# Two output tiles of one chunk stored by one transfer, and a hand-written instruction order replaced by another

## The chip, the cores and the metric

The kernel runs on one core of one Trainium2 chip. A core has TensorE (matmuls and transposes, called PE in the profile; PEld is its loading of weights), VectorE (DVE), ScalarE (ACT), GpSimd (POOL) and SyncE (SP), each with an instruction stream of its own, and 16 DMA engines that all queues share. The metric is the time of the core on the device in microseconds (us), the median over the runs. Before the change it is 308.44 us.

## The reference

It is causal attention over a sliding window, followed by a two-layer network. Cut to what is computed:

```python
# q, k, v: (8 batches, 8 heads, 576 tokens, 64), float32
scores = q @ k.transpose / 8
scores = where(0 <= row - column < 64, scores, -1e9)
attn   = exp(scores - max) / sum            # softmax over columns
y      = attn @ v
x      = y as (8 * 576 = 4608 tokens, 8 * 64 = 512)
h      = x @ w_in                           # 512 x 2048
g      = h - tanh(h)
out    = g @ w_out                          # 2048 x 512, out is (4608, 512) float32
```

## The kernel before

**Tiling.** A batch has 576 tokens, which are nine windows of 64; a window's queries look at 128 keys, its own and those of the window ahead. Heads are taken in pairs: a *group* g is batch g // 4 and pair g % 4, so groups 0 to 3 are batch 0 and groups 4 to 7 are batch 1. The network works on nine *chunks* of 512 tokens, so chunk 0 needs batch 0 alone, and the network of one chunk runs on TensorE between the attention of later batches. All matmul operands are bf16 and all sums are float32. PSUM is one tile `ps` of eight banks, and each step of the program names the bank that it uses.

**The order.** Nothing is scheduled by a planner: the kernel turns automatic scheduling off and plays one long string of words, `PLAN`, from left to right. `play` splits a word at its dots and calls the helper that `STEPS` gives for it. So the string fixes the order of instructions on every engine and in every DMA queue; what waits for what between engines follows from which helper reads or writes which tile, and of two words whose spans of a tile overlap the later one in the string waits for the earlier one. The words that matter here, with g a group, c a chunk, and a final `.a`, `.v`, `.p` or `.s` for ScalarE, VectorE, GpSimd or SyncE:

- `lq.g`, `lk.g` (L107): load the q or k rows of one group; `.p` goes through GpSimd's queue, `.s` through SyncE's. `LV.b.i` (L142) loads 128 value rows of batch b with all heads, `lv` one head's value rows, `wi` and `wo` weights of the two layers; all these go through GpSimd's queue.
- `cq.g`, `ck.g` (`move`, L87 on ScalarE and L89 on VectorE): cast and reorder a group's rows to bf16.
- `Ep.g.bank`, `Fp.g.bank`: transpose q or k of a group on TensorE into a bank, in six matmuls where the rows were cast before (L252) and in twelve where not (L248). `Ec`, `Fc`: copy the result out of PSUM, on ScalarE or VectorE.
- `U.n.bank` (L219): n warm-up matmuls on a tile of zeros, whose result nobody reads; 512 columns wide, in bank 7 only 384.
- `Rp.g.grp.bank`: scores of a group for its first five (grp 0) or last four (grp 1) windows, into two banks. For groups 0 to 3 two matmuls that write the mask come first (L273). Bank 4 here stands for the banks 4 and 7. `Rx` is the exp of them on ScalarE (L310).
- `Z.b` (L148 and L149): two copies on VectorE by which value rows cross to the other half of the partitions; the weighted sums read them.
- `P.g` (L327): weighted sums of a group of batch 0, which also give the softmax's denominators; they lie in banks 5 and 6, for group 2 in banks 0 and 1. `D.g` (L367 and L369) is the reciprocal and the product that divide them; `DS` and `DH` are the same in parts for group 2. From batch 1 on two groups go together: `PP` (L340), `DR` and `DN`.
- `Xp`, `Xc` (L389 and `move`): transpose the divided sums on TensorE to the layout of a token chunk, and copy them out.
- `Hp` (L495) and `H` (L423): the first layer, 128 of the 2048 hidden columns at a time, in two halves of two matmuls or in four matmuls at once; `A` the tanh (L431, ScalarE), `G` the subtraction (L437, VectorE), `W` the second layer (L466; L459 for the last 128 tokens).
- `O.c.s` (`y_out`): copy 128 tokens' outputs of chunk c out of PSUM into a tile `ysb`, and store them with a transfer on SyncE's queue (L482). The last 128 tokens go in two parts, 384 and 128 columns wide (L477).

SyncE issues 105 transfers: two loads of rows (`lq.0.s`, `lk.0.s`), 66 DMA transposes of later batches, and 37 outputs. They use eight completion counters in turn, number n the counter (n - 1) mod 8, so that transfer 105 is on counter 0 and transfer 104 on counter 7; a transfer waits for the one eight before it, whose counter it takes over. At the end of the program SyncE waits for GpSimd's queues, then for its own counters 0 to 7 in this order, one instruction for each, and only then the program drains and ends (L633).

Of the kernel before, what the change touches and what calls it, by code (L numbers as in the profile page):

```python
# [15 lines left out]
def kernel(  # L16
# [68 lines left out]
    def move(eng, o, i):
        if eng is nc.scalar:
            nc.scalar.activation(o, i, ACT.Copy)  # L87
# [381 lines left out]
    def y_out(c, s, eng):  # L469
        if c == NC or (c, s) == (NC - 1, 3):  # L470
            half = c - NC + 1
            c, s = NC - 1, 3
# [4 lines left out]
            nc.sync.dma_start(out=out[r0:r0 + 128, d], in_=ysb[:, d])  # L477
# [41 lines left out]
    def play(script):  # L519
# [15 lines left out]
        Fc.6.4.v H.0.3 Ec.5.5.a cq.6.v Ep.6.5 G.0.1 Fc.5.3.a N A.0.3 Ec.6.5.v G.0.3 Rp.4.0.6 Rp.5.1.3 Hp.0.2.1  # L535
        lv.1.0.1 H.0.4 ck.8.v wi.4 Rx.5.1.3 A.0.2 A.0.4 Rx.4.0.6 G.0.2 H.0.6 H.0.5 A.0.6 Rp.6.1.4 mz Rp.6.0.5
        lq.8.p G.0.4 cq.7.v lv.1.3.1 A.0.5 zb.1.1.p lt.1 wo.0 H.0.7 Rx.6.1.4 zb.1.0.p Ep.7.3 Rx.6.0.5 Fp.7.4
        lv.1.2.0 lv.1.3.0 Rp.5.0.5 wo.2 A.0.7 G.0.5 H.0.8 M.4 G.0.6 H.0.9 G.0.7 za.1.1.p H.0.10 Ec.7.3.a
        Rx.5.0.5 Fc.7.4.v lk.9.p A.0.8 G.0.8 A.0.9 za.1.0.a H.0.11 A.0.10 Fp.8.5 A.0.11 Rp.7.1.3 M.6 G.0.9
        Rp.7.0.6 Rx.7.0.6 H.0.12 Fc.8.5.a G.0.10 G.0.11 wo.3 A.0.12 H.0.14 cq.8.v Ep.8.1 M.5 PP.4 G.0.12 A.0.14  # L540
        H.0.15 G.0.14 Ec.8.1.a A.0.15 DR.4 Rx.7.1.3 DN.4.0 H.0.13 DN.4.1 G.0.15 W.0.0.0 DN.4.2 M.7 za.1.2.a
        zb.1.2.v zb.1.3.p Rp.8.0.3 Rp.8.1.5 A.0.13 Rx.8.1.5 W.0.1.0 wo.1 lq.10.p lk.10.p lq.11.p za.1.3.v
        lk.11.p PP.6 G.0.13 cq.9.v Rx.8.0.3 LV.2.0 DR.6 Xp.1.0.0.3 lr.3.2 Xp.1.0.1.4 qr.3.3 W.0.1.2 Xc.1.0.1.4.v
        DN.6.1 W.0.0.2 Xc.1.0.0.3.a ck.9.v DN.6.0 DN.6.2 Fp.9.3 Hp.1.0.0 Ep.9.4 Xp.1.1.0.6 Xp.1.1.1.7 Fc.9.3.a
# [10 lines left out]
        qr.4.1 LV.3.4 Xc.2.0.1.3.a A.1.14 DN.10.0 W.1.0.0 G.1.14 LV.4.3 lr.4.1 W.1.0.2 A.1.15 Xp.2.1.1.4
        Xp.2.1.0.6 LV.4.2 W.1.0.1 LV.4.0 G.1.15 W.1.0.3 Xc.2.1.1.4.a Xc.2.1.0.6.a lr.4.0 qr.5.3 Hp.2.0.0
        Hp.2.0.1 A.2.0 qr.4.4 qr.5.4 H.2.3 tk.4.4 lr.6.4 qr.4.0 O.1.0.v A.2.3 W.1.1.3 G.2.3 W.1.1.2 lr.4.2
        Hp.2.1.1 Hp.2.1.0 G.2.0 lr.5.4 lr.5.2 H.2.2 qr.4.3 lr.4.3 A.2.1 S.12 W.1.1.0 LV.4.4 A.2.2 G.2.1 tq.4.4
        H.2.5 G.2.2 W.1.1.1 Sx.12.2 tq.4.0 Sx.12.1 Sx.12.0 A.2.5 Z.3 M.12 H.2.4 M.13 O.1.1.a A.2.4 qr.4.2 G.2.5
        PP.12 W.1.2.3 tq.4.1 tk.4.1 DR.12 G.2.4 tk.4.0 tk.4.2 DN.12.1 DN.12.2 H.2.7 DN.12.0 tk.4.3 tq.4.3 lr.6.3  # L560
        qr.5.2 lr.5.3 lr.5.0 H.2.6 S.14 lr.5.1 qr.5.0 qr.6.4 A.2.7 A.2.6 G.2.7 qr.6.0 H.2.9 Sx.14.2 Sx.14.0
        tq.4.2 A.2.9 Sx.14.1 G.2.6 G.2.9 M.14 W.1.2.2 W.1.2.1 W.1.2.0 H.2.8 H.2.11 M.15 A.2.8 G.2.8 PP.14
        Xp.3.0.0.4 A.2.11 DR.14 O.1.2.v H.2.10 Xp.3.0.1.3 W.1.3.3 W.1.3.2 A.2.10 DN.14.0 DN.14.1 G.2.10 G.2.11
        DN.14.2 H.2.12 A.2.12 H.2.13 W.1.3.0 W.1.3.1 A.2.13 Xp.3.1.1.7 G.2.12 G.2.13 H.2.15 Xp.3.1.0.6 O.1.3.a
        Xc.3.0.0.4.a H.2.14 Xc.3.1.1.7.a A.2.15 A.2.14 W.2.0.2 G.2.14 Xc.3.1.0.6.v G.2.15 W.2.0.0 W.2.0.1
        Xc.3.0.1.3.a tq.5.3 tq.5.4 tk.5.4 tz.4.v tq.5.2 Hp.3.0.1 W.2.0.3 Hp.3.1.1 Hp.3.1.0 O.2.0.a A.3.1 W.2.1.1
        Hp.3.0.0 W.2.1.2 G.3.1 A.3.0 S.16 Z.4 Sx.16.1 Sx.16.2 G.3.0 Sx.16.0 M.17 M.16 H.3.3 W.2.1.3 W.2.1.0
        H.3.2 A.3.3 PP.16 G.3.3 O.2.1.a DR.16 A.3.2 qr.5.1 H.3.5 LV.5.3 tk.5.2 G.3.2 DN.16.2 DN.16.0 tk.5.1
        tk.5.3 DN.16.1 tq.5.0 A.3.5 W.2.2.1 Y.4.0 H.3.4 S.18 A.3.4 Sx.18.0 G.3.5 H.3.7 G.3.4 A.3.7 G.3.7 Sx.18.1
        Sx.18.2 H.3.6 A.3.6 W.2.2.3 W.2.2.0 M.19 H.3.9 W.2.2.2 tk.6.4 tq.5.1 tk.5.0 G.3.6 qr.7.1 M.18 H.3.8  # L570
        A.3.9 PP.18 A.3.8 O.2.2.v G.3.9 DR.18 G.3.8 DN.18.2 DN.18.0 W.2.3.0 H.3.11 qr.6.2 DN.18.1 LV.5.4 A.3.11
        lr.6.2 W.2.3.3 W.2.3.1 H.3.10 W.2.3.2 A.3.10 G.3.11 G.3.10 Y.4.1 lr.6.0 tq.6.4 tq.6.2 O.2.3.a H.3.13
        H.3.14 A.3.13 LV.5.0 LV.5.1 LV.5.2 W.3.0.2 lr.6.1 qr.6.1 G.3.13 H.3.15 tz.5.v A.3.14 G.3.14 qr.6.3
        H.3.12 W.3.0.0 A.3.15 G.3.15 Hp.4.1.0 A.3.12 G.3.12 Hp.4.1.1 A.4.1 Hp.4.0.1 W.3.0.1 G.4.1 W.3.0.3 H.4.3
# [63 lines left out]
```

## Time and profile before

| | us |
|---|---|
| median of three runs | 308.44 |
| the three runs | 307.77, 308.44, 308.54 |
| the profiled execution | 308.71 |
| span of its profile (first to last instruction) | 307.0 |
| TensorE, matmuls busy | 298.4 |
| VectorE busy | 176.4 |
| ScalarE busy | 155.6 |
| GpSimd busy | 104.3 |

The granted clock of TensorE is 0.998 of full speed in the mean over the profiled execution. TensorE's matmuls cover 97% of the span. The largest groups of its time are the second layer's matmuls, 130.1 us, and the first layer's, 120.9 us and 20.9 us for those in halves; the 35 warm-ups are 10.8 us.

The rows that follow below have these forms. A row of the timeline gives the start, the busy time of the run of equal instructions, the engine, the line of the kernel, the operation, written tile <- read tiles, the shapes, and how many there are; the bracket is the idle time of that engine ahead of them and what ended it. A row of the windows gives the bounds of a stretch, its length, and each engine's busy time in it with the number of instructions, then TensorE's granted clock, the mean share of DMA engines in use (above 1 where transfers queue), and the rate in GB/s. In a row of a view of groups stand the count, the shortest, median and longest single time in ns, and the first and last start.

### The profile page before, as it was taken

The numbers are of one execution on the slowest core, as the hardware profiler recorded it, in microseconds if no ns is written. First come the engines' busy times: TensorE is split into PE (matmuls) and PEld (weight loads), VectorE is DVE, ScalarE is ACT, GpSimd is POOL, SyncE is SP. The second block draws the span as 40 slices with busy tenths as digits, with TensorE's granted clock in tenths as the row PEclk, the third lists the DMA queues.
The fourth block names the chain that finished last, engine by engine and source line by source line (L and its number), as shares of the span: only waits on it lengthen the run. The fifth ranks groups of instructions, "written<-read, shape, count | busy, mean of one in ns | idle before, by whom it ended". The sixth has DMA issues, their size and how long they took to land.

```text
span 307.0 us, 6473 instructions
## 1 busy us (share of the span) xinstructions
PE 298.4 (97%) x2599; PEld 149.5 (49%) x2632; DVE 176.4 (57%) x312; ACT 155.6 (51%) x263; POOL 104.3 (34%) x141
## 2 busy tenths in 40 slices
PE   8989999999999999999999999999999999999995
PEld 3555555455555545444544445444544444444443
DVE  1378995389577636765386575576663645355300
ACT  2668983577665356634464645345733433433202
POOL 8988756830979092038005870000000000000000
PEclk9999999999999999999999999999999999999999
DMA  8999999998999999969999999650032000001102
GB/s 161 153 191 193 186 192 176 160 188 123 115 150 136 176 154 138 184 108 144 178 139 125 144 173 128 144 99 34 36 75 73 35 36 34 34 34 36 67 35 104
DMA packets 132894, 36.77 MB, mean 120 GB/s; under 512 B 119936, under 2 KB 127360, under 8 KB 132864
## 3 DMA queue, kind: packets, MB, share of 16 engines
q0 software_dynamic: 92752, 18.06, 82.3%
q1 hardware_dynamic: 40112, 18.30, 30.9%
q8 instruction: 20, 0.33, 0.5%
q14 instruction: 10, 0.08, 0.1%
...
## 4 chain that ended last, share of the span: by engine, by line
PE 90%; DVE 2%; DMA 2%; POOL 2%; issue 1%; ACT 1%; DVEq 0%; ACTq 0%; POOLq 0%
PE ps L466 39%; PE ps L423 35%; PE ps L495 6%; PE ps L340 3%; DMA vw<-in_v_dram 2%; PE ps L296 2%; PE ps L389 1%; PE ps L252 1%; PE ps L459 1%; PE ps L278 1%; DVE xs L369 1%; POOL qall L107 1%; POOL vw L142 1%; POOL kall L107 1%; DVE gT L437 0%
## 5 line engine op out<-in xcount | busy, mean ns | idle before, releaser
L437 DVE TENSOR_TENSOR gT<-ps,th 128x512 bf16<-128x512 f32 x144 | 97.1, 686 | 79.7 <-ACT th L431 79.0
L431 ACT ACTIVATE th<-ps 128x512 f32<-128x512 f32 x144 | 85.2, 599 | 95.7 <-PE ps L423 78.2
L466 PE MATMUL ps<-w_out_sb,gT 128*128 128x512 bf16 x527 | 130.1, 379 | 2.2 <-issue 0.8
L423 PE MATMUL ps<-xT,wi 128*128 128x512 bf16 x496 | 120.9, 379 | 0.1
L466 PEld LDWEIGHTS <-gT 128*128 128x128 bf16 x560 | 53.7, 98 | 62.9
L423 PEld LDWEIGHTS <-wi 128*128 128x128 bf16 x496 | 46.9, 98 | 54.7 <-issue 0.8
L142 POOL DMA_DIRECT2D vw<-in_v_dram x35 | 30.5, 886 | 37.3 <-PE ps L340 32.9
L87 ACT ACTIVATE ysb<-ps 128x512 f32<-128x512 f32 (+2 forms) x24 | 13.9, 580 | 31.7 <-PE ps L466 30.5
L158 POOL DMA_DIRECT2D qall<-in_q_dram x25 | 21.6, 882 | 17.7 <-DMA qw<-qall 17.0
L158 POOL DMA_DIRECT2D kall<-in_k_dram x25 | 21.5, 870 | 13.9 <-DMA kw<-kall 11.0
L306 ACT ACTIVATE pt<-ps 128x1024 bf16<-128x1024 f32 (+1 forms) x30 | 23.1, 814 | 3.0 <-PE ps L296 2.7
L315 DVE TENSOR_TENSOR pt<-pt,ps 128x1152 bf16<-128x1152 bf16 x28 | 20.4, 747 | 3.6 <-ACT pt L306 3.5
L495 PE MATMUL ps<-xT,wi 128*128 128x512 bf16 x80 | 20.9, 379 | 0.0
L310 ACT ACTIVATE pt<-ps 128x640 bf16<-128x640 f32 (+1 forms) x24 | 15.0, 651 | 3.7 <-PE ps L278 2.3
L360 DVE TENSOR_TENSOR xs<-ps,rcp 128x384 bf16<-128x384 f32 x28 | 14.9, 548 | 0.2
L89 DVE COPY ysb<-ps 128x512 f32<-128x512 f32 x13 | 8.9, 682 | 9.9 <-PE ps L466 9.9
L219 PE MATMUL ps<-warm 128*128 128x512 bf16 (+1 forms) x35 | 10.8, 451 | 1.3 <-DVE warm L199 1.1
L340 PEld LDWEIGHTS <-pt 128*64 128x64 bf16 x504 | 9.2, 111 | 4.9 <-ACT th L431 1.7
L495 PEld LDWEIGHTS <-wi 128*128 128x128 bf16 x80 | 7.3, 98 | 7.7 <-DVE xT L89 0.2
L340 PE MATMUL ps<-vw,pt 128*64 128x65 bf16 x504 | 10.8, 197 | 0.0
L87 ACT ACTIVATE xT<-ps 128x512 bf16<-128x512 bf16 (+3 forms) x14 | 6.4, 508 | 3.6 <-PE ps L389 3.6
L357 DVE TENSOR_TENSOR xs<-ps,rcp 128x384 bf16<-128x384 f32 x14 | 7.7, 549 | 0.0
...
## 6 DMA issues: line engine op xcount, KB each, us to landing
out_dram<-ysb SPq DMA_DIRECT2D x35, 256.0 KB, 2.3
vw<-in_v_dram POOLq DMA_DIRECT2D x28, 128.0 KB, 6.7
kall<-in_k_dram POOLq DMA_DIRECT2D x20, 128.0 KB, 6.8
qall<-in_q_dram POOLq DMA_DIRECT2D x20, 128.0 KB, 7.2
...
```

The source lines that it names most:

```text
L87: nc.scalar.activation(o, i, ACT.Copy)
L142: nc.gpsimd.dma_start(out=w[:, 2 * i + 1, :, 0:D] if i < NF else w[64:128, 2 * i, :, 0:D], in_=v[b, :, 128 * i:128 * i + n].rearrange("h p ...
L158: nc.gpsimd.dma_start(out=token_rows(b, n)[0:c, i], in_=(q if n == "q" else k)[b, :, 128 * i:128 * i + c].rearrange("h p d -> p h d"))
L306: nc.scalar.activation(o, sp, ACT.Exp, scale=scale)
L310: nc.scalar.activation(PT[g % NPT][:, js[0]:js[0] + len(js), :].rearrange("p i (h t) -> p i h t", h=2), sp, ACT.Exp, scale=scale)
L315: nc.vector.tensor_tensor(p, p, mask.unsqueeze(1).to_broadcast([128, 2 * NJ, 64]), ALU.mult)
L340: nc.tensor.matmul(ps[r, bank, 65 * i:65 * i + 65], PT[(g + r2) % NPT][:, j, r], vw[b % 2][:, j, p0 + r2 + NP * h, :], start=True, stop=True)
L423: nc.tensor.matmul(hp, w_in_tile(ki, m), chunk_tile(c)[:, n.start // 64:n.stop // 64, ki % 2, 64 * (ki // 2):64 * (ki // 2) + 64], start=( ...
L431: nc.scalar.activation(th[:, n], hp, ACT.Tanh)
L437: nc.vector.tensor_tensor(gT[c][:, m, columns(s)], hp, th, ALU.subtract)
L466: nc.tensor.matmul(yp, gT[c][:, m, s * 128:(s + 1) * 128], w_out_sb[:, m, :], start=n == 1 and i == 0, stop=n == 4 and i == 3)
L495: nc.tensor.matmul(hp, w_in_tile(half + 2 * i, m), chunk_tile(c)[:, :, half, 64 * i:64 * i + 64], start=n == 1 and i == 0, stop=n == 2 and ...
```

## The change

It has two parts. The first is in `y_out`: outputs of the first 256 tokens of chunk 6 (`O.6.0` and `O.6.1`) no longer go through two `ysb` tiles and two transfers of 256 KB each. Both copies write halves of a tile of their own, `two`, and the second of them is followed by one transfer of 512 KB. SyncE has 104 transfers then, the last one on counter 7, and SyncE's order has one instruction fewer from that place on.

The second is the string: its first 570 words of 1171 are in a new order, and the words from `tz.4.v` on, which are played from about 113 us on, are as before. Both strings hold the same real steps; some steps have another PSUM bank, some copies go to the other engine (ScalarE has three instructions more, VectorE three copies fewer), and the 35 warm-ups stand at other places: 24 come ahead of the first transpose where 27 did. Among what moves:

- the loads: four value loads `LV.0` and the last queries and keys of batch 0 change places, and `lk.4`, `lk.5`, `lq.4` come behind the last value load;
- `D.0` stands ahead of `Rx.2.0.4` and not behind it;
- `Ec.1.0` is on ScalarE, behind `Fc.2.1`; it was on VectorE;
- `Fp.6.3` stands ahead of the first layer's first step, `Hp.0.0.0`; `Fp.6.4` stood behind `Hp.0.0.1`;
- `LV.3.3` stands behind `LV.4.1`; it stood far ahead of it.

The lines of the changed kernel are 3 higher up to L466 (L327 is L330, L466 is L469) and 8 higher behind the new branch (the store of whole tiles at L482 is L490, the first layer's halves at L495 are L503, the end of the program at L633 is L641); the last tile's store, L477, is L480, and the joined transfer is L485.

```diff
@@ -80,6 +80,9 @@
+    JOINED = 6
+    two = const.tile([128, 2, d_model], F32, name="two")
...
@@ -476,6 +479,11 @@
+        if c == JOINED and s < 2:
+            move(eng, two[:, s], ps[:, yp_bank(c, s), :])
+            if turn("y", c) == 2:
+                nc.sync.dma_start(out=out[c * TOK:c * TOK + 256].rearrange("(s p) d -> p s d", p=128), in_=two)
+            return
         ysb = sm_pool.tile([128, d_model], F32, tag="ysb", name="ysb")
         move(eng, ysb, ps[:, yp_bank(c, s), :])
...
@@ -522,89 +530,89 @@
     PLAN = """
-        lq.1.p u mv.0 mt.1 mv.1 mt.3 lq.2.p lq.3.p U.1.0 U.1.3 lk.1.p lk.0.s lk.3.p U.1.1 U.1.7 U.4.0 U.1.3
-        U.1.5 lk.2.p LV.0.2 U.4.0 lq.0.s cq.0.a LV.0.1 LV.0.0 U.1.6 i LV.0.3 U.1.4 U.1.7 U.1.4 U.4.1 U.1.0 U.1.1
-        U.1.3 U.1.1 U.1.7 Ep.2.3 LV.0.4 Ep.1.0 lk.4.p Ep.0.4 Ec.1.0.v Fp.1.5 U.1.6 Fp.3.1 U.1.2 lq.6.p Ec.2.3.v
-        Ep.3.0 Fc.1.5.v h Ec.0.4.a ck.0.a Fp.2.2 lq.4.p Fp.0.4 U.1.7 mt.0 Ec.3.0.a Fc.0.4.v Fc.2.2.a Rp.1.0.5
-        Fc.3.1.a Z.0 mt.2 Rx.1.0.5 Rp.3.0.4 Rp.3.1.1 Rx.3.0.4 Rp.1.1.5 lk.6.p Rp.0.1.4 lk.5.p wi.1 wi.0 lv.1.1.0
-        Rx.3.1.1 lk.7.p Rp.0.0.2 lq.5.p Rx.1.1.5 Rx.0.1.4 ck.4.a P.1 Rx.0.0.2 D.1 Rp.2.1.0 Rp.2.0.4 Rx.2.1.0 P.0
-        Rx.2.0.4 U.1.3 cq.4.v U.1.0 U.1.0 D.0 P.2 Fp.4.7 DS.2 DH.2.1 DH.2.0 ck.6.a U.1.6 P.3 Ep.4.1 D.3
-        Xp.0.0.0.2 wi.2 Xc.0.0.0.2.a U.1.0 ck.5.v Xp.0.0.1.4 lv.1.2.1 Fc.4.7.a Xc.0.0.1.4.v Xp.0.1.0.5 Fp.5.3
-        Xp.0.1.1.2 lk.8.p lq.7.p lv.1.0.0 Ec.4.1.a Xc.0.1.1.2.v n lv.1.1.1 wi.3 Xc.0.1.0.5.a ck.7.v lq.9.p
-        Hp.0.0.0 cq.5.v Hp.0.1.0 Hp.0.0.1 Fp.6.4 Hp.0.1.1 A.0.0 Rp.4.1.6 A.0.1 G.0.0 Hp.0.2.0 Ep.5.5 Rx.4.1.6
...
-        W.0.2.0 O.0.2.v W.0.3.2 W.0.3.0 Hp.1.1.1 O.0.3.a qr.3.1 Fp.10.6 LV.3.3 Hp.1.1.0 Hp.1.2.1 Ep.11.4
...
-        PP.10 LV.4.1 LV.3.1 G.1.12 G.1.13 DR.10 LV.3.0 LV.3.2 Xc.2.0.0.4.a lr.4.4 tz.3.a H.1.15 DN.10.1 DN.10.2
...
+        u lq.3.p lq.1.p lk.3.p U.4.7 U.1.2 U.1.3 mt.0 i lq.2.p U.4.1 U.1.4 lq.0.s U.1.4 mv.0 U.1.5 U.1.1 U.1.3
+        U.1.2 U.1.1 lk.2.p U.1.0 lk.1.p LV.0.1 mt.3 U.1.7 U.1.1 U.4.0 lk.0.s mt.2 ck.0.a Ep.3.7 Ec.3.7.a LV.0.0
+        Fp.3.5 Fp.0.6 U.1.1 cq.0.v mt.1 Fc.3.5.v LV.0.2 Ep.1.0 U.1.2 U.1.3 U.1.3 Ep.2.2 Fc.0.6.v Ep.0.4 U.1.3
+        LV.0.3 Fp.2.1 Fp.1.3 U.1.7 LV.0.4 Ec.0.4.a lk.4.p Fc.2.1.a lk.5.p Fc.1.3.v h Ec.1.0.a U.1.7 Ec.2.2.v
+        mv.1 lq.4.p Rp.1.0.5 Rp.1.1.0 Rp.3.1.4 Rx.1.0.5 Rx.1.1.0 Rp.3.0.5 Z.0 Rp.0.0.2 Rp.0.1.0 Rx.3.1.4
+        Rx.3.0.5 Rx.0.0.2 P.1 lk.6.p Rp.2.1.2 wi.1 wi.0 Rx.0.1.0 lq.5.p Rp.2.0.4 D.1 cq.4.v P.0 lv.1.1.0
+        Rx.2.1.2 lk.7.p lq.6.p U.1.1 D.0 Rx.2.0.4 ck.4.a ck.6.a P.2 wi.2 Ep.4.3 lv.1.1.1 P.3 DS.2 DH.2.0 D.3
+        U.1.7 U.1.4 Ec.4.3.a ck.5.a Xp.0.0.0.2 Fp.4.4 Xp.0.0.1.0 U.1.7 DH.2.1 Xc.0.0.1.0.a Fc.4.4.a Xp.0.1.0.5
+        Fp.5.6 Xp.0.1.1.7 lk.8.p Fp.6.3 lq.7.p lv.1.0.0 Xc.0.0.0.2.v n Xc.0.1.0.5.v lv.1.2.1 Xc.0.1.1.7.v
+        Fc.6.3.a Hp.0.0.0 Fc.5.6.v Hp.0.0.1 wi.3 A.0.0 cq.5.v Hp.0.2.0 cq.6.v Hp.0.1.0 lv.1.0.1 lt.1 Ep.5.4
...
+        LV.4.1 tq.3.3 LV.3.3 G.1.13 A.1.14 H.1.15 A.1.15 Xc.2.0.1.4.a LV.3.0 LV.3.1 DR.10 DN.10.0 DN.10.2 LV.3.2
...
```

More of the change, by code (lines that the diff above doesn't have):

```diff
@@ L535 @@
[L535 to L544, printed above, removed]
@@ L555 @@
[L555 to L564, printed above, removed]
@@ L565 @@
[L565 to L574, printed above, removed]
@@ new lines @@
+        W.2.3.1 H.3.10 W.2.3.2 A.3.10 G.3.11 G.3.10 Y.4.1 lr.6.0 tq.6.4 tq.6.2 O.2.3.a H.3.13 H.3.14 A.3.13
+        LV.5.0 LV.5.1 LV.5.2 W.3.0.2 lr.6.1 qr.6.1 G.3.13 H.3.15 tz.5.v A.3.14 G.3.14 qr.6.3 H.3.12 W.3.0.0
+        A.3.15 G.3.15 Hp.4.1.0 A.3.12 G.3.12 Hp.4.1.1 A.4.1 Hp.4.0.1 W.3.0.1 G.4.1 W.3.0.3 H.4.3 Hp.4.0.0
+        O.3.0.v tk.6.2 A.4.0 S.20 A.4.3 Sx.20.1 Sx.20.0 tk.6.0 tk.6.3 tq.6.0 G.4.0 Sx.20.2 G.4.3 W.3.1.1 W.3.1.0
+        H.4.2 W.3.1.3 A.4.2 S.22 G.4.2 H.4.4 W.3.1.2 H.4.7 A.4.4 G.4.4 M.20 O.3.1.a Sx.22.0 Sx.22.1 A.4.7
@@ new lines @@
+        lr.7.1 W.4.0.2 G.4.15 A.4.14 Hp.5.1.0 G.4.14 Hp.5.1.1 LV.7.2 lr.7.4 Sx.24.1 W.4.0.3 Hp.5.0.1 Hp.5.0.0
+        lr.7.3 A.5.1 G.5.1 O.4.0.a A.5.0 H.5.3 G.5.0 A.5.3 M.25 qr.7.4 W.4.1.0 W.4.1.3 H.5.2 qr.7.2 LV.7.4
+        LV.7.3 G.5.3 M.24 A.5.2 W.4.1.2 W.4.1.1 Z.6 G.5.2 H.5.5 O.4.1.a PP.24 lr.7.0 LV.7.0 A.5.5 H.5.4 DR.24
+        A.5.4 DN.24.0 G.5.5 tq.7.0 W.4.2.3 G.5.4 DN.24.2 H.5.7 DN.24.1 H.5.6 S.26 tk.7.4 A.5.6 tq.7.4 G.5.6
+        Sx.26.0 A.5.7 Y.6.0 W.4.2.0 W.4.2.1 tk.7.2 H.5.8 tq.7.3 G.5.7 W.4.2.2 H.5.9 Sx.26.2 tk.7.0 tk.7.1
@@ new lines @@
+        Sx.26.1 A.5.8 G.5.8 A.5.9 H.5.10 O.4.2.v W.4.3.0 W.4.3.1 M.26 G.5.9 tk.7.3 tq.7.2 H.5.11 W.4.3.2 A.5.11
+        M.27 G.5.11 PP.26 W.4.3.3 DR.26 A.5.10 DN.26.0 G.5.10 O.4.3.a H.5.13 H.5.12 tz.7.v DN.26.1 DN.26.2
+        W.5.0.1 A.5.13 A.5.12 G.5.13 G.5.12 H.5.15 H.5.14 Y.6.1 A.5.15 W.5.0.0 W.5.0.2 A.5.14 S.28 Z.7 G.5.14
+        G.5.15 W.5.0.3 Hp.6.1.0 Hp.6.1.1 Hp.6.0.0 O.5.0.v Sx.28.2 W.5.1.1 W.5.1.2 Sx.28.1 A.6.1 G.6.1 Hp.6.0.1
+        M.29 Sx.28.0 M.28 A.6.0 H.6.3 G.6.0 W.5.1.3 A.6.3 H.6.2 G.6.3 A.6.2 G.6.2 H.6.5 PP.28 H.6.4 A.6.5
@@ L608 @@
+        W.8.3.2 O.8.2.a O.9.0.a W.8.3.0 W.8.3.1 O.8.3.a"""
     play(PLAN)
```

97 lines of the change are left out of this document (56 added, 41 removed).

## The prediction

> **What bounds the kernel now.** I read the page's busy shares and its chain of waits first, then the windows by stage, then the timeline of the first 28 us, then SyncE's last instructions.
>
> ```profile
> span 307.0 us, 6473 instructions
> PE 298.4 (97%) x2599; PEld 149.5 (49%) x2632; DVE 176.4 (57%) x312; ACT 155.6 (51%) x263; POOL 104.3 (34%) x141
> PE 90%; DVE 2%; DMA 2%; POOL 2%; issue 1%; ACT 1%; DVEq 0%; ACTq 0%; POOLq 0%
> ```
> ```profile
> core 0: us, PE busy (x) PEld busy (x) DVE busy (x) ACT busy (x) POOL busy (x), PEclk, DMA share, GB/s
> 10.00:24.00 14.00, 12.59 (x267) 8.00 (x265) 9.27 (x21) 10.51 (x18) 12.03 (x22) 1.00 1.76 175
> 24.00:45.00 21.00, 20.94 (x246) 11.09 (x244) 19.08 (x37) 18.71 (x35) 14.59 (x23) 1.00 1.40 190
> 250.00:300.00 50.00, 49.79 (x231) 22.83 (x235) 18.52 (x28) 15.58 (x27) 0.00 (x0) 1.00 0.11 42
> 300.00:307.00 7.00, 3.21 (x29) 2.04 (x27) 0.00 (x0) 1.37 (x3) 0.00 (x0) 0.93 0.31 114
> ```
> From 24 us to the last matmul TensorE is never idle to speak of (20.94 of 21, 49.79 of 50), and the change leaves every real matmul in place. So time is won or lost in two places only: how much real TensorE work is done by about 24 us, and what follows the last matmul. Between them an order can lose, but hardly gain.
>
> **The tail (gain 0.8 us).** SyncE's last two transfers and what its instruction stream does after them:
>
> ```profile
> L477 SPq DMA_DIRECT2D out_dram<-ysb x2: 332/332/333, 302.9 to 303.6; - x2
> DMA to landing us min/median/max: 1.6/1.7/1.9
> L633 SPq EVENT_SEMAPHORE  x8: 27/28/28, 305.2 to 306.0; - x8
> L633 SPq DRAIN  x1: 33/33/33, 306.1 to 306.1; - x1
> ```
> The last transfer is issued at 303.6 and lands 1.6 us later, at 305.2. Transfers take eight completion counters in turn, and the closing sequence waits for counters 0 to 7 in that order, one instruction each. Transfer 105 is on counter 0, so the first of these eight holds all the others: they run only from 305.2 to 306.0. With 104 transfers the last is on counter 7, the last one waited for. Seven waits then fall into the 1.6 us while that transfer is under way, and one is left: 306.0 - 305.2 = 0.8 us less. The eight stand 0.11 us apart on average though each lasts 28 ns, so part of the 0.8 may be a stall of the stream at one place, which could remain. Bounds: half of it, 0.4, and 0.85. I take 0.8, because SyncE idles through the landing and can spend such a stall there.
>
> The joined transfer itself costs nothing:
> ```profile
> out_dram<-ysb SPq DMA_DIRECT2D x35, 256.0 KB, 2.3
> ```
> Its two copies out of PSUM stay (same shapes, same engine); half the data leaves one output step later, and 512 KB at twice 2.3 us is 4.6 us. Behind it on SyncE stand only later outputs; it is issued some 35 us before the end. If that cover were gone the price would be the extra 2.3 us.
>
> **The opening (loss 0.6 us).** The timeline of before, from the warm-up matmuls (L219) over the first batch's weighted sums P.1, P.0, P.2, P.3 (L327) and their divisions D (L367, L369) to the first layer (L495):
>
> ```profile
> 1.06 8.07 PE L219 MATMUL ps<-warm 128*128 128x512 bf16 x27 [1.06 <-DVE warm L199]
> 5.62 3.07 PEld L219 LDWEIGHTS <-warm 128*128 128x128 bf16 x15 [0.28 <-issue]
> 9.06 0.70 PE L248 MATMUL ps<-ident,qall 96*64 96x96 bf16 x24
> 12.49 1.19 ACT L87 ACTIVATE kt<-ps 128x576 bf16<-128x576 bf16 x2
> 12.52 0.43 PE L273 MATMUL ps<-hide,ident 128*128 128x320 bf16 x2
> 13.55 1.81 ACT L310 ACTIVATE pt<-ps 128x640 bf16<-128x640 f32 x3
> 16.33 0.79 DVE L149 COPY vw<-vw 64x2080 bf16<-64x2080 bf16 x1
> 17.17 0.51 PE L327 MATMUL ps<-vw,pt 128*64 128x65 bf16 x20 [0.48 <-DVE vw L149]
> 17.61 0.39 PE L273 MATMUL ps<-hide,ident 128*128 128x256 bf16 x2
> 17.79 0.22 DVE L367 RECIPROCAL rc<-ps 128x10 f32<-128x10 f32 x1 [0.52 <-PE ps L327]
> 18.05 0.82 DVE L369 TENSOR_TENSOR xs<-ps,rc 128x640 bf16<-128x640 f32 x1
> 18.16 0.45 PE L273 MATMUL ps<-hide,ident 128*128 128x320 bf16 x2
> 18.92 0.51 PE L327 MATMUL ps<-vw,pt 128*64 128x65 bf16 x20
> 19.46 0.70 ACT L310 ACTIVATE pt<-ps 128x640 bf16<-128x640 f32 x1 [0.60 <-PE ps L327]
> 20.07 0.83 ACT L87 ACTIVATE kb<-kall 96x768 bf16<-96x768 bf16 x1
> 20.20 0.22 DVE L367 RECIPROCAL rc<-ps 128x10 f32<-128x10 f32 x1 [1.07 <-ACT pt L310]
> 20.22 0.51 PE L327 MATMUL ps<-vw,pt 128*64 128x65 bf16 x20
> 21.64 0.51 PE L327 MATMUL ps<-vw,pt 128*64 128x65 bf16 x20
> 22.09 0.43 PE L252 MATMUL ps<-ident,qb 96*128 96x96 bf16 x6
> 22.35 0.39 PE L389 MATMUL ps<-ident,xs 128*128 128x128 bf16 x4
> 22.58 0.38 PE L219 MATMUL ps<-warm 128*128 128x512 bf16 x1
> 24.14 1.46 PE L495 MATMUL ps<-xT,wi 128*128 128x512 bf16 x6
> 25.43 0.42 PE L252 MATMUL ps<-ident,kb 96*128 96x96 bf16 x6
> 31.16 0.53 PEld L423 LDWEIGHTS <-wi 128*128 128x128 bf16 x3 [0.29 <-issue]
> ```
> (a) Up to P.1. It waits for the crossing of the value rows (L149, done 17.1), which waits for the fourth value load. After still issues six query and key loads and the five value loads first, and the DMA share of 1.76 in this window says that they queue; so P.1 stays at 17.17. But its other cover gets thin. After has 24 warm-ups before the first transpose instead of 27, five of them narrow: that ends near 8.3, against 9.06. Then the way to the first scores (3.46 us before, 9.06 to 12.52) holds seven warm-ups instead of three, 4 x 0.216 more: 12.65. Those scores read the copies of Fp.1.3 and Ec.1.0, which now comes last on ACT, behind Fc.2.1: two copies of 1.19 us together from about 12.2, so 13.4. Four groups of scores at 0.55 (17.61 to 18.16) reach 15.6; the exps Rx.3.1.4 and Rx.3.0.5, 0.6 and 0.7, free P.1's banks at 16.9. That is 0.2 us of cover; value loads that land early give P.1 at most 0.26.
>
> (b) P.1 to P.2, the step that decides. Group Rx.2.0.4 lies in banks 4 and 7, and the wait that the program takes for it spans banks 4 to 7, those of D.0 among them: whichever comes first in the plan is waited for by the other. Before, the exp is first: P.0 18.92, exp 19.46 to 20.16, P.2 20.22, and D.0 idles 1.07 us for it. After, D.0 is first: its reciprocal 0.6 after P.0's start (as 17.17 to 17.79), 19.5; product 19.76 to 20.58; the exp 20.63 to 21.33; P.2 at 21.38, 1.16 later.
>
> (c) P.2 to the first layer. Before this takes 3.92 us, 20.22 to 24.14, with waits in it for D.0 and for the last division. After, TensorE's own list runs it without them, each by the distance of starts in the rows (P 17.17 to 17.61, Ep and Fp 22.09 to 22.35, Xp of four 22.35 to 22.58): P.2 0.44, Ep.4.3 0.26, P.3 0.54 with 0.1 for the change of kind, two warm-ups 0.48 likewise, Xp 0.23, Fp.4.4 0.25, Xp of five 0.28, narrow warm-up 0.16, Xp 0.23, Fp.5.6 0.25, Xp 0.28, Fp.6.3 0.25 = 3.65: Hp.0.0.0 at 25.03. ACT, which it also waits for, has three casts of 0.83 (20.07) and three copies of 0.6, 0.6 and 0.3 behind the exp of 0.70: 20.63 + 4.69, less the 0.09 by which neighbours overlap (19.46 + 0.70 against 20.07) six times, is 24.8. Fp.6.3 is real work that before has behind Hp.0.0.1 (25.43, 0.26). Loss: 25.03 - 24.14 - 0.26 = 0.63. If all of P.2's delay passed on it would be 1.16; if none, 0, and 0.26 gained with early loads. I take 0.6.
>
> (d) Before, H.0.5 lost about 0.17 us at 31.16 (0.29 idle where 0.12 is usual); VectorE, less pressed against a later TensorE, should not cause that again: -0.17, bound 0.
>
> **28 to 113 us.** The rest of the new order is costed at nothing: no real matmul is added, and TensorE's backlog hides it. Three evacuations move from DVE to ACT, some 0.6 us each; where ACT is fullest it has 2.3 us free in 21. The one moved load whose cover I checked is LV.3.3, now behind LV.4.1, so that the last load before the crossing for batch 3 is fifth and not fourth in its row:
> ```profile
> 77.36 3.50 POOL L142 DMA_DIRECT2D vw<-in_v_dram  x4 [13.18 <-PE ps L340]
> vw<-in_v_dram POOLq DMA_DIRECT2D x28, 128.0 KB, 6.7
> 88.72 0.85 DVE L148 COPY vw<-vw 64x2080 bf16<-64x2080 bf16 x1
> ```
> Issued at 77.36 + 3.50 = 80.9, it lands by 87.6 at the median 6.7: 1.1 us before the crossing at 88.72. Past that each us is lost, since VectorE's products of later tiles queue behind it. Bounds for this stage: -0.1 and +1.8 (three 0.6 us copies, uncovered).
>
> **Sum.** -0.8 + 0.63 - 0.17 = -0.34 us on the profiled execution's own 308.71 us (span 307.0): 308.4. That execution is 0.27 above the median of the runs, 308.44, so the forecast for the median is 308.1.
>
> **The cold start.** The first twelve warm-ups start 0.43 us apart, the fifteen weight loads from 5.62 on take 0.2 each, so the rate doubles 4.6 us after the first. The Trainium skill ("TensorE: Matmul & The Clock Gate", Part 1: The HAM clock gate) says that the budget is time and not a number of matmuls, about 3.4 us, and that its window runs free, so that the count of slow ones differs from run to run. By that rule the switch could come later in the changed kernel too, and the 0.2 us of cover in (a) would not hold; by the row it comes at 5.6 again and the sum stands.
>
> **The rivals.**
> 1. Faster: the loss in (b) is hidden, because the order of before idles as much elsewhere (D.0 waits 1.07 us there), and loads land early: 308.44 - 0.8 - 0.17 - 0.26 = 307.2. For: 10 to 24 us has 1.4 us of TensorE idle and warm-ups besides. Against: P.2 is on the path in both, and (c) leaves after no waits to remove.
> 2. Slower: P.1 loses its cover. If the slow clock lasts until the warm-ups are over, the last 11 cost 0.21 more each, 2.3 us; beyond 0.2 all of it reaches P.1, so 308.1 + 2.1 = 310.2. It decides from first transposes later than 8.5 us. For: only 0.2 us of cover. Against: the rows show the switch at 5.6, with 11 warm-ups still to come.
> 3. The change does not do what it says: the closing waits still stand in a row behind the last landing, or the stall among them moves with them. Then -0.8 is lost: 308.9.
> 4. ACT becomes the bound after 28 us: 308.1 + 1.8 = 309.9. For: 18.71 busy of 21. Against: most of the moved copies come after 45 us, where it has room.
>
> **How the numbers follow.** Forecast 0.44, rivals 0.30, 0.10, 0.10 and 0.06. About 0.3% (0.93 us) is what a measurement of this kernel tells from no change. The forecast (-0.34) and rival 3 (+0.46) fall mostly within it; rival 1 (-1.2) is faster, 2 and 4 are slower. With 0.04 of the forecast's chance beyond the bound on the fast side and 0.02 of rival 3's on the slow: faster 0.34, within 0.48, slower 0.18. Range: down to rival 1, 307.2; up to -0.4 + 1.16 on 308.44, 309.2, with a tenth for jitter: 309.3. Rivals 2 and 4 lie outside.
>
> **What would show it.** In the profile after: one EVENT_SEMAPHORE of line 641 behind the last landing instead of eight, and about 0.8 us from landing to drain less; P.1 near 17.2, P.2 near 21.4 with its exp released by VectorE; the first layer (L503) near 25.0; TensorE 99% busy from there. The forecast is wrong if P.2 starts before 20.8, if P.1 slips past 17.4, if the row of waits remains, or if windows between 28 and 113 us show TensorE idle.

## The result, and the profile after

The changed kernel takes 310.19 us (median of 19 runs, 308.68 to 313.33) where the kernel before takes 308.54 (19 runs, 307.43 to 309.63): a ratio of 1.0059, 95% interval 1.0038 to 1.0081. It is slower by 1.7 us; the forecast was 308.1 in a range of 307.2 to 309.3. The 19 runs fall apart by the mean granted clock of TensorE that stands beside each:

| mean granted clock | runs | us | median |
|---|---|---|---|
| 1.000 or 0.999 | 4 | 308.68 to 309.82 | 308.8 |
| 0.994 | 8 | 309.72 to 310.51 | 310.0 |
| 0.989 | 3 | 310.94 to 311.28 | 311.3 |
| 0.983 or 0.984 | 4 | 311.99 to 313.33 | 312.6 |

The steps are nearly equal, 1.2 to 1.3 us for each 0.005 or 0.006 of clock. The profiled execution is one of 0.994; it took 310.10 us with a span of 308.4. Its page, with the busy shares and the chain of waits:

```profile
span 308.4 us, 6489 instructions
PE 300.8 (98%) x2632; PEld 149.9 (49%) x2632; DVE 175.9 (57%) x309; ACT 156.7 (51%) x266; POOL 104.0 (34%) x141
PE 92%; DMA 2%; POOL 2%; DVE 1%; issue 1%; ACT 1%; ACTq 0%; DVEq 0%; POOLq 0%
```

TensorE still bounds the kernel, now with 92% of the chain in place of 90%. Its busy share says little of the loss: a matmul that takes longer at a lower clock counts as busy for longer, and the 97% of before lacks 33 matmul records (x2599, where x2632 weights were loaded). Where the clock went is seen in the windows of the opening, TensorE alone (bounds, length, busy time with matmuls, granted clock, DMA share, GB/s):

```profile
14.60:18.00 3.40, 2.20 (x56) 1.00 1.39 182
18.00:21.40 3.40, 1.88 (x43) 1.00 1.49 193
21.40:24.80 3.40, 3.21 (x53) 0.50 1.31 203
24.80:28.20 3.40, 3.40 (x43) 1.00 1.66 182
28.00:45.00 17.00, 16.68 (x202) 1.00 1.36 201
45.00:70.00 25.00, 25.00 (x239) 1.00 2.06 173
70.00:113.00 43.00, 43.00 (x437) 1.00 1.65 126
```

For 3.4 us, from 21.4 to 24.8, TensorE runs at half its clock, and in the 3.4 us ahead of it it had worked for 1.88. One such interval is 0.5 x 3.4 / 308.4 = 0.0055 of the mean clock, so by this arithmetic the rows of the table are runs with none, one, two and three of them; only a run with one was profiled. A mean of 0.997 to 0.999 can have another source: the profile of before (0.998) loses its share behind the last matmul, where nothing is left to slow down (its row from 300 to 307 us, ahead in the prediction, has 0.93). The timeline shows what TensorE waited for and what the half clock did:

```profile
17.36 0.51 PE L330 MATMUL ps<-vw,pt 128*64 128x65 bf16 x20 [1.20 <-DVE vw L152]
...
19.12 0.51 PE L330 MATMUL ps<-vw,pt 128*64 128x65 bf16 x20
19.55 0.39 PE L222 MATMUL ps<-warm 128*128 128x512 bf16 x1
19.66 0.22 DVE L370 RECIPROCAL rc<-ps 128x10 f32<-128x10 f32 x1 [0.33 <-PE ps L330]
19.91 0.82 DVE L372 TENSOR_TENSOR xs<-ps,rc 128x640 bf16<-128x640 f32 x1
20.83 0.70 ACT L313 ACTIVATE pt<-ps 128x640 bf16<-128x640 f32 x1 [1.77 <-DVE xs L372]
21.59 0.76 PE L330 MATMUL ps<-vw,pt 128*64 128x65 bf16 x20 [1.65 <-ACT pt L313]
...
22.88 0.78 PE L330 MATMUL ps<-vw,pt 128*64 128x65 bf16 x20
...
26.50 1.89 PE L503 MATMUL ps<-xT,wi 128*128 128x512 bf16 x8
...
36.38 0.42 PE L255 MATMUL ps<-ident,kb 96*128 96x96 bf16 x6 [0.32 <-ACT pt L313]
```

P.1, P.0, P.2 and P.3 are the four rows of L330. The chain from P.0 over D.0 (L370, L372) and the exp to P.2 is the one that the prediction laid out, 0.2 us later. TensorE is empty for 1.65 us ahead of P.2, and P.2 itself takes 0.76 where the twenty matmuls of P.1 and of P.0 took 0.51 each. The first layer starts at 26.50; before, it was 24.14. The last row is a stall that before did not have: Fp.7.4, the transpose of group 7 into bank 4, waits 0.32 us for an exp that reads this bank.

The end of the program, SyncE's last transfers and closing instructions:

```profile
L480 SPq DMA_DIRECT2D out_dram<-ysb x2: 332/332/332, 305.2 to 305.9; - x2
DMA to landing us min/median/max: 1.6/1.7/1.9
...
L641 SPq EVENT_SEMAPHORE  x8: 27/28/28, 306.3 to 307.1; - x8
...
L641 SPq DRAIN  x2: 7/7/7, 307.6 to 307.6; - x2
L641 SPq EVENT_SEMAPHORE  x1: 28/28/28, 307.5 to 307.5; - x1
```

The last transfer lands 1.6 us after 305.9, at 307.5. Eight closing waits are through by then, at 307.1 (by the order of the closing sequence one for GpSimd's queues, which came at 304.0 in before, and those for counters 0 to 6), and one is left. From landing to the end of the span it is 0.92 us, where it was 1.80.

So the span's change of +1.44 us has three parts: the first layer starts 2.36 us later (26.50 against 24.14), from there to the end of TensorE's last matmul nothing changes (279.02 against 279.06), and from the last landing to the end it is 0.88 us less. All of the loss lies ahead of 26.5 us.

### The profile page after: what moved, and what is told of

Same layout as the page of the kernel before. It is cut to its first block, busy times and chain, and to the rows that moved or that the text cites. A ratio compares the mean times of both kernels' runs of the same rounds, so it can differ in the third digit from the quotient of the medians.

```text
span 308.4 us, 6489 instructions
## 1 busy us (share of the span) xinstructions
PE 300.8 (98%) x2632; PEld 149.9 (49%) x2632; DVE 175.9 (57%) x309; ACT 156.7 (51%) x266; POOL 104.0 (34%) x141
## 4 chain that ended last, share of the span: by engine, by line
PE 92%; DMA 2%; POOL 2%; DVE 1%; issue 1%; ACT 1%; ACTq 0%; DVEq 0%; POOLq 0%
PE ps L469 40%; PE ps L426 35%; PE ps L503 6%; PE ps L343 3%; DMA vw<-in_v_dram 2%; PE ps L299 2%; PE ps L255 1%; PE ps L392 1%; PE ps L462 1%; PE ps L281 1%; PE ps L330 1%; POOL kall L110 1%; POOL qall L110 1%; POOL vw L145 1%; DVE xs L372 1%
## 5 line engine op out<-in xcount | busy, mean ns | idle before, releaser
L469 PE MATMUL ps<-w_out_sb,gT 128*128 128x512 bf16 x560 | 134.5, 379 | 0.0
L469 PEld LDWEIGHTS <-gT 128*128 128x128 bf16 x560 | 53.6, 98 | 62.5
L161 POOL DMA_DIRECT2D qall<-in_q_dram x25 | 21.7, 881 | 16.5 <-DMA qw<-qall 15.6
L503 PE MATMUL ps<-xT,wi 128*128 128x512 bf16 x80 | 20.5, 379 | 0.0
L363 DVE TENSOR_TENSOR xs<-ps,rcp 128x384 bf16<-128x384 f32 x28 | 14.9, 550 | 0.2
L503 PEld LDWEIGHTS <-wi 128*128 128x128 bf16 x80 | 7.5, 98 | 8.3
L92 DVE COPY ysb<-ps 128x512 f32<-128x512 f32 x10 | 6.8, 681 | 6.1 <-PE ps L469 6.1
L90 ACT ACTIVATE xT<-ps 128x512 bf16<-128x512 bf16 (+3 forms) x16 | 7.1, 499 | 2.3 <-PE ps L392 2.2
L110 POOL DMA_DIRECT2D qall<-in_q_dram x11 | 7.4, 677 | 2.1 <-POOLq L630 0.9
```

Of the source, the lines that this page charges most:

```text
L161: nc.gpsimd.dma_start(out=token_rows(b, n)[0:c, i], in_=(q if n == "q" else k)[b, :, 128 * i:128 * i + c].rearrange("h p d -> p h d"))
L363: nc.vector.tensor_tensor(xs[b % 2][:, p0 // 2, 0:6, n // 2, :], ov[:, :, 0:D], sums[g][:, n].to_broadcast([128, 6, D]), ALU.mult)
L469: nc.tensor.matmul(yp, gT[c][:, m, s * 128:(s + 1) * 128], w_out_sb[:, m, :], start=n == 1 and i == 0, stop=n == 4 and i == 3)
L503: nc.tensor.matmul(hp, w_in_tile(half + 2 * i, m), chunk_tile(c)[:, :, half, 64 * i:64 * i + 64], start=n == 1 and i == 0, stop=n == 2 and ...
```

## The experiments

Each kernel was run beside the kernel before; the times of before in these three groups of runs are 308.68, 308.54 and 308.54. "P.2 at 21.59" is a start in a timeline, the first row of its kind.

**The joined transfer alone.** The code of the change in the kernel before, with the old string:

```diff
...
+        if c == JOINED and s < 2:
+            move(eng, two[:, s], ps[:, yp_bank(c, s), :])
...
```

> The kernel before with the joined transfer and nothing else. If the tail gain is real and as large as the row of closing waits (0.8 us), the median is 307.7 against 308.5 of before, one closing wait of SyncE stands behind the last landing, and TensorE's part is as before. If the stall among the waits moves with them, the gain is 0.4 and the median 308.1; if joining brings nothing, 308.5. All of the slowdown is then the order's.

Measured: 308.17 us (12 runs) against 308.68, ratio 0.9985 (0.9972 to 0.9999). Closing waits behind the last landing, in its list of SyncE's instructions:

```profile
L641 SPq DRAIN  x2: 7/68/130, 305.0 to 305.3; - x2
L641 SPq EVENT_SEMAPHORE  x1: 28/28/28, 304.9 to 304.9; - x1
```

One wait is left, as expected. But the two DRAINs stand 0.35 us apart where the changed kernel has them 0.05 apart, and landing to end takes 1.34 us. So this kernel gains 0.46 us at its end, and its median is the one expected for a stall that moves along (308.1). By these two profiles the join is worth 0.46 or 0.88, by whether there is such a stall. It gains in both; the slowdown is the order's.

**The new order alone.**

```diff
-    JOINED = 6
+    JOINED = -1
```

> The changed kernel with the two transfers of before (105 in all), so the new order alone. Against the changed kernel's 310.2 the tail gives back 0.8: 311.0 in the mean over its clock states; runs in which the granted clock stays at 1.00 should take 309.5 (308.7 + 0.8). If the join brought nothing, 310.2.

Measured: 310.81 us (6 runs), ratio 1.0060 (1.0040 to 1.0079); one run at clock 1.00 with 309.44, the others at 0.992 to 0.994 with 310.33 to 311.70. Its eight waits run behind the last landing again (1.82 us to the end). Both times are within 0.2 of what was expected of a tail gain of 0.8.

**The exp ahead of D.0**, the changed kernel with the old order of these two words:

```diff
-        Rx.2.1.2 lk.7.p lq.6.p U.1.1 D.0 Rx.2.0.4 ck.4.a ck.6.a P.2 ...
+        Rx.2.1.2 lk.7.p lq.6.p U.1.1 Rx.2.0.4 D.0 ck.4.a ck.6.a P.2 ...
```

> The changed kernel with the exp Rx.2.0.4 ahead of D.0, as before. Theory (the wait of P.2 for D.0 opens a gap of 1.65 us in TensorE, its busy share in one 3.41 us interval of the clock falls to 0.55, and the clock is halved for the next interval): P.2 comes near 20.4 instead of 21.6, the gap shrinks to some 0.5 us, the granted clock is 1.00 in most runs and the time is 307.9. Rival (the gap of 1.2 us ahead of P.1 is what trips the clock): clock 0.994 and lower remain in most runs, and the time falls only by P.2's own delay, to 309.2. Rival (the loss is the longer chain of waits up to the first layer, the clock a side effect of it): the first layer starts as late as in the changed kernel, 26 or later, and the time stays at 310.

Measured: 307.88 us (12 runs), ratio 0.9983 (0.9966 to 1.0001); ten runs at 0.999 or 1.00, two at 0.994. From its timeline:

```profile
19.82 0.70 ACT L313 ACTIVATE pt<-ps 128x640 bf16<-128x640 f32 x1 [0.60 <-PE ps L330]
...
20.58 0.51 PE L330 MATMUL ps<-vw,pt 128*64 128x65 bf16 x20 [0.47 <-ACT pt L313]
...
24.47 1.89 PE L503 MATMUL ps<-xT,wi 128*128 128x512 bf16 x8
```

The exp (first row) is released by TensorE and not by VectorE, P.2 comes one us earlier, and the first layer two us earlier. (It still waits 0.60 us for P.0, whose banks 5 and 6 lie within the span of banks 4 to 7.) One word's place is the whole slowdown, and more: the kernel is 2.3 us faster for it. The next run tells how much of the two us is the clock's part.

**Warm-ups in the gap.** All waits stay as in the changed kernel; seven more warm-up matmuls stand in the time in which TensorE waits:

```diff
-        ... U.1.1 D.0 Rx.2.0.4 ck.4.a ck.6.a P.2 ...
+        ... U.1.1 D.0 Rx.2.0.4 ck.4.a ck.6.a U.7.1 P.2 ...
```

> The changed kernel with seven more warm-up matmuls (1.5 us) between P.0 and P.2, where TensorE waits; all waits stay as they are. Theory (clock): P.2 stays at 21.6, the gap ahead of it shrinks to 0.2 us, the clock stays at 1.00 in most runs and the time falls to 308.7, which is what the changed kernel takes in its runs at clock 1.00. Rival (the gap ahead of P.1): clock 0.994 stays in most runs, 310. Rival (the wait itself is the loss): the time stays at 310.2 whatever the clock does.

Measured: 308.58 us (12 runs), ratio 1.0000 (0.9976 to 1.0025); ten runs at 0.999 or 1.00, two at 0.994. Its timeline:

```profile
19.54 1.90 PE L222 MATMUL ps<-warm 128*128 128x512 bf16 x8
21.58 0.51 PE L330 MATMUL ps<-vw,pt 128*64 128x65 bf16 x20
...
25.16 1.89 PE L503 MATMUL ps<-xT,wi 128*128 128x512 bf16 x8
```

Its windows, TensorE alone:

```profile
20.00:23.40 3.40, 3.27 (x59) 1.00 1.40 188
23.40:26.80 3.40, 3.40 (x45) 1.00 1.46 193
```

P.2 starts at the same time as in the changed kernel, so the wait is untouched; yet it takes 0.51 again, and the first layer comes at 25.16 and not at 26.50. This is the run that separates the two costs: 1.02 us for the new order and its waits (25.16 against 24.14), 1.34 us for the clock (26.50 against 25.16). Of the two us by which the exp's place moves the first layer, 0.69 are the chain's (25.16 against 24.47) and 1.34 the clock's. Seven matmuls on zeros, which compute nothing, win 1.6 us of the median.

**Warm-ups in both gaps**, five more (`U.5.4`) ahead of P.1 besides the seven.

```diff
-        Rx.3.0.5 Rx.0.0.2 P.1 lk.6.p ...
+        Rx.3.0.5 Rx.0.0.2 U.5.4 P.1 lk.6.p ...
```

> The changed kernel with warm-ups in both gaps of TensorE, five (1.1 us) ahead of P.1 and seven (1.5 us) ahead of P.2; all waits stay. Theory (a gap halves the clock by the busy share that it leaves in an interval of 3.41 us): no interval is left below 0.85, so that no run shows a granted clock of 0.994 or lower, and the median is that of the filled kernel's runs at clock 1.00, 308.4. Rival (the two slow runs of twelve in the kernel with seven warm-ups came from elsewhere, the cold start or the first layer's stage): runs at 0.994 stay about as often, and the median is 308.6.

Measured: 309.02 us (12 runs), ratio 1.0015 (1.0002 to 1.0028). The clock is 0.999 or 1.00 in all twelve, as expected, but the time is 0.6 above the expectation and 0.4 above the kernel with the seven alone. In the four kernels that have the five warm-ups P.1 starts between 17.57 and 18.01, in the changed kernel and the five with its order of loads and without them between 17.32 and 17.67. In two of the four P.1 starts right behind the warm-ups, so that it waits for them; in the other two it waits for the value rows, which came later there. A part of the 0.4 is the filler's own, then, and how much was not settled.

**Warm-ups ahead of P.1 alone.** The same edit in the changed kernel without the seven.

> The changed kernel with five warm-ups ahead of P.1 alone; the gap of 1.65 us ahead of P.2 stays empty. Theory: the second gap trips the clock by itself, so more than half of the runs show 0.994, the median is 309.9; runs at 0.989 and 0.984 become rarer if those come of both gaps in one run. Rival (the first gap is the cause): clock 1.00 in nearly all runs, 308.6. Rival (it takes both gaps): clock 1.00 in more than two thirds of the runs.

Measured: 310.68 us (6 runs), ratio 1.0063 (1.0046 to 1.0081), all six at 0.994. Windows of its opening:

```profile
19.40:22.80 3.40, 1.69 (x55) 1.00 1.39 183
22.80:26.20 3.40, 3.40 (x44) 0.50 1.36 190
```

The gap ahead of P.1 is closed and the clock falls all the same, in every run, behind the gap ahead of P.2. That rules the first gap out as the cause of one slow interval. Runs with two and three of them, 7 of 19 in the changed kernel, did not occur here; six runs are few to say that they need both gaps.

**D.0 first in the old order**, one word moved in the kernel before:

```diff
-        Rx.2.0.4 U.1.3 cq.4.v U.1.0 U.1.0 D.0 P.2 ...
+        D.0 Rx.2.0.4 U.1.3 cq.4.v U.1.0 U.1.0 P.2 ...
```

> The kernel before (105 transfers) with one word moved: D.0 ahead of Rx.2.0.4. If the moved wait is the loss in any order, P.2 starts near 21.3 instead of 20.2. Three warm-ups stand in the gap there, which leaves some 1.2 us empty. By the chain of waits alone the first layer starts 0.4 to 1.1 us later than in before and the time is 309.0 to 309.6 against 308.6, with the clock at 1.00 in most runs; if a gap of 1.2 us is enough for the clock, half of the runs are at 0.994 and the median is 310.2. Rival (the old order has room for it, since D.0 comes earlier than before): 308.6, no change.

Measured: 309.52 us (12 runs) against 308.54, ratio 1.0032 (1.0018 to 1.0045); eleven runs at 0.997 or above, one at 0.993. From its timeline, and from the windows of the gap and of its end:

```profile
21.12 0.51 PE L327 MATMUL ps<-vw,pt 128*64 128x65 bf16 x20 [1.22 <-ACT pt L310]
...
24.82 1.46 PE L495 MATMUL ps<-xT,wi 128*128 128x512 bf16 x6
```
```profile
19.10:22.60 3.50, 2.28 (x54) 1.00 1.47 193
...
302.50:305.90 3.40, 1.55 (x21) 1.00 0.43 154
305.90:307.80 1.90, 0.00 (x0) 1.00 0.01 4
```

The word costs 1.0 us in the old order too, by the chain of waits alone: P.2 0.90 later than in before, the first layer 0.68. With three warm-ups in it the gap is 1.22 us, and the clock holds.

**The same without the three warm-ups.**

```diff
-        D.0 Rx.2.0.4 U.1.3 cq.4.v U.1.0 U.1.0 P.2 ...
+        D.0 Rx.2.0.4 cq.4.v P.2 ...
```

> The kernel before with D.0 ahead of Rx.2.0.4 and without the three warm-ups between P.0 and P.2, so that the same late P.2 leaves TensorE empty for about 1.8 us. Theory (clock by busy share): the granted clock is 0.994 in most runs, and the time is 1.3 above the 309.5 of the same order with its three warm-ups: 310.8. Rival (the clock of the changed kernel falls for something else in its order, the thinner warm-up at the start or the casts): clock 1.00 and 309.5, since the chain of waits is the same and the warm-ups do nothing.

Measured: 309.60 us (12 runs), ratio 1.0044 (1.0024 to 1.0065). The median is the rival's (309.5) and not the theory's (310.8); the clock is between the two: seven runs at 0.998 or 0.999 with 309.00 to 309.66, four at 0.994 with 310.02 to 310.43, one at 0.984 with 312.53. The profiled execution is one at 0.994:

```profile
18.00:21.40 3.40, 1.37 (x50) 1.00 1.52 192
21.40:24.80 3.40, 3.40 (x54) 0.50 1.35 200
```
```profile
21.10 0.59 PE L327 MATMUL ps<-vw,pt 128*64 128x65 bf16 x20 [1.97 <-ACT pt L310]
```

The profile shows a slow interval behind the gap in the old order as well, but it comes in five runs of twelve and not in most. With the three warm-ups one run of twelve had it, and in the kernel before 5 of the 79 runs beside these experiments had a clock of 0.993 or 0.994; five of twelve against one of twelve are too few runs to call a difference. The gap is the longest of all, 1.97 us; whether an interval catches it whole depends on where the intervals fall in a run, which the runs do not tell outside the profile. The theory's "most runs" was wrong.

**One warm-up in the gap**, with five ahead of P.1.

```diff
-        ... ck.4.a ck.6.a P.2 ...
+        ... ck.4.a ck.6.a U.1.1 P.2 ...
```

> The changed kernel with five warm-ups ahead of P.1 and one more ahead of P.2, so that the second gap shrinks from 1.65 to about 1.4 us and the worst interval of the clock goes from 0.50 busy (the run without this warm-up, six of six runs at 0.994) to about 0.56. Theory (the busy share of one interval decides, with a bound between 0.55 and 0.64 by the profiles so far): some runs at 0.994 and some at 1.00, by where the free interval falls, median between 309.0 and 310.7. Rival (any gap of over a us does it): all runs at 0.994, 310.7. Rival (it takes 1.6 us or more): all at 1.00, 309.0.

Measured: 310.34 us (9 runs), ratio 1.0045 (1.0028 to 1.0063): six runs at 0.994, three at 0.999 or 1.00 with 309.59 to 309.77. Its windows:

```profile
19.20:22.60 3.40, 1.90 (x58) 1.00 1.47 194
22.60:26.00 3.40, 3.40 (x44) 0.50 1.38 198
```

With 1.43 us of gap some runs fall and some don't. The intervals can be counted off in every profile, since those at half clock begin a whole number of 3.413 us behind the rise of the clock at the start, to within 0.1 us: in the changed kernel weight loads stand 0.2 us apart from 4.41 on, and 4.41 + 5 x 3.413 = 21.5; in before from 5.62 on, and 5.62 + 88 x 3.413 = 306.0, where the clock is halved behind the last matmul. By the fourteen profiles, an opening interval in which TensorE was busy for 0.56 of the time or less was followed by half clock (five profiles), and one with 0.64 or more never was.

**The exp first, and warm-ups ahead of P.1**: the two edits shown above in one kernel.

> The changed kernel with the exp Rx.2.0.4 ahead of D.0 and five warm-ups ahead of P.1. Theory: of the two causes of low busy shares in that stage both are gone, all runs are at clock 1.00, the tail's gain stays, and the median is 307.7, 0.9 below before and 0.2 below the kernel with the exp first alone, whose two slow runs of twelve vanish. If those came from elsewhere: 307.9.

Measured: 308.14 us (12 runs), ratio 0.9982 (0.9968 to 0.9995), all twelve at 0.999 or 1.00. The clock is as expected; the time is 0.4 above the 307.7 of the expectation and no better than with the exp first alone (307.88), since P.1 starts at 18.01 here, right behind the last warm-up, and the value rows that it needs were there at 16.7.

**Other banks for group 2**, so that none of its exps shares a span of banks with D.0, in the changed kernel; with them both exps stand ahead of D.0 (lines cut and broken anew):

```diff
-        ... P.1 lk.6.p Rp.2.1.2 wi.1 wi.0 Rx.0.1.0 lq.5.p Rp.2.0.4 D.1 cq.4.v P.0 lv.1.1.0
-        Rx.2.1.2 lk.7.p lq.6.p U.1.1 D.0 Rx.2.0.4 ck.4.a ck.6.a P.2 ...
+        ... P.1 lk.6.p Rp.2.0.2 wi.1 wi.0 Rx.0.1.0 lq.5.p Rp.2.1.0 D.1 cq.4.v Rx.2.0.2 P.0 lv.1.1.0
+        Rx.2.1.0 lk.7.p lq.6.p U.1.4 D.0 ck.4.a ck.6.a P.2 ...
```

> The changed kernel with group 2's scores in the banks 2-3 and 0-1 in place of 4/7 and 2-3, so that neither of its exps shares a span of banks with D.0; both exps now stand ahead of D.0, and the one warm-up there goes to bank 4. If the wait between exp and D.0 was what held P.2, P.2 starts near 19.7, right behind P.0, P.3 near 20.9 (it waits for D.0), the clock stays at 1.00 and the first layer comes at 23.6 against 24.5 of the kernel with the exp first: 307.0 to 307.3, faster than before and than all kernels so far. If ScalarE's casts and copies hold the first layer anyway, it comes at 24.3 and the time is 307.8.

Measured: 307.14 us (6 runs, 306.77 to 307.61) against 308.54, ratio 0.9949 (0.9931 to 0.9967), all at 0.999 or 1.00. Its timeline:

```profile
18.58 1.19 ACT L313 ACTIVATE pt<-ps 128x640 bf16<-128x640 f32 x2 [0.98 <-PE ps L281]
...
19.91 0.51 PE L330 MATMUL ps<-vw,pt 128*64 128x65 bf16 x20
...
20.83 0.51 PE L330 MATMUL ps<-vw,pt 128*64 128x65 bf16 x20
...
23.61 1.89 PE L503 MATMUL ps<-xT,wi 128*128 128x512 bf16 x8
```

P.2 follows P.0 and a warm-up with nothing between, both exps are through by 19.8, and the first layer starts at 23.61, the number that was expected. This is faster than before and than the changed kernel: 1.4 and 3.1 us. Of the 3.1 the exp's place ahead of D.0 brings 2.3 (the run with the exp first, 307.88); the other 0.7 come with the banks and with the places of the exps that they allow, where neither waits for P.0. The kernel before has the same waits (its exp waits 0.60 us for P.0, its D.0 1.07 us for the exp, and P.2 is at 20.22); what other banks are worth in the old order was not run.

**Two joined transfers**, 103 in all, on the kernel with the exp first:

```diff
...
-        if c == JOINED and s < 2:
+        if c == JOINED:
...
-            if turn("y", c) == 2:
+            if turn("y", c) % 2 == 0:
...
```

> The changed kernel with the exp first and all four output tiles of chunk 6 in two joined transfers, so 103 in all and the last on counter 6. If the closing waits stand in the order of the counters, two of them follow the last landing (0.07 us apart) where one does with 104 and eight with 105, and landing to end takes 0.99 us against 0.92. If the gain had come of the transfer count in another way, landing to end falls further or stays. The time is 307.9 within 0.7 (one look).

Measured: 308.23 us in one run; landing to end 0.99 us, as expected to the hundredth.

```profile
L642 SPq EVENT_SEMAPHORE  x7: 28/28/28, 304.2 to 305.0; - x7
...
L642 SPq EVENT_SEMAPHORE  x2: 28/28/28, 305.4 to 305.5; - x2
```

Seven waits stand ahead of the landing, two behind: with the last transfer on counter 6, one wait more than with counter 7, 0.07 us. The time is one run's and says little.

## Why the prediction was wrong, point by point

- **The tail** was right in its mechanism and nearly in its size: 0.88 us in place of 0.8, a little beyond the bound of 0.85, shown by the two kernels that take one part each and by the counter that moved by one. The bound of 0.4 that the prediction kept for a stall that moves along was needed too: the join in the old order gained 0.46.
- **(a) Up to P.1** was right: 17.36 against 17.17, released by the crossing of the value rows. The first scores came at 12.58, where 13.4 was forecast, so the cover was thicker than thought and the exps never held P.1.
- **(b) P.1 to P.2**, the wait of the exp for D.0, was right in its mechanism and to 0.2 us (21.59 against 21.38); the kernel with the exp first and the one with other banks show that this wait is what delays P.2.
- **(c) P.2 to the first layer** is the step that failed. It said that TensorE's list runs "each by the distance of starts in the rows" to 3.65 us, and put the first layer at 25.03. It took 4.91 us, and 26.50. The distances came from rows at full clock, and (b) had just left TensorE empty for 1.65 us; the interval ahead of P.2 was 55% busy, and the clock was halved for the next 3.4 us, which covers (c) up to 24.8. With the gap filled by warm-ups the same list took 3.58 us and the first layer came at 25.16: the sum of starts was right to 0.1, its clock was wrong. That is 1.34 us in the profile, and about 1.3 us for each such interval in the runs. The prediction had no term and no rival for it.
- **The cold start** looked at the right mechanism in the wrong place. It asked whether the clock would rise later than the 5.6 us of before, and it rose at 4.4 (the weight loads stand 0.2 us apart from there on). It did not ask whether a gap in the middle could make it fall again. Rival 2 has the price of the result (310.2) but not its cause: P.1 was not late, and the first transposes came at 7.68, ahead of the 8.5 from which that rival decided.
- **(d) and 28 to 113 us** were mis-sized. The stall of 0.17 at H.0.5 is gone, and Fp.6.3 is done ahead of the first layer, which together should have saved 0.43 us behind its start. Behind it, before and after take the same 279.0 us. A new stall of 0.32 at 36.38 (Fp.7.4 waits for the exp Rx.6.1.4, which reads the same bank and now stands two words ahead of it where it stood four ahead) takes three quarters of it back; the rest is spread too thin to name. The late load LV.3.3 and the copies on ScalarE cost nothing: TensorE is busy for 43.00 of 43 us from 70 to 113.
- **The sum**, term by term on the profiled executions: -0.34 forecast; +0.13 for (a) to (c) at full clock, +1.34 for the clock, +0.39 for what (d) and Fp.6.3 did not bring, -0.08 at the tail: +1.44, which is 308.4 against 307.0. Without the slow interval the result is within 0.3% of before: the four runs at clock 1.00 have a median of 308.8, within the forecast's range, 0.7 above the forecast.
